# Batch 1's loads and w1 in one GpSimd queue; V_bf's evacuation and one norm placed elsewhere

## The chip, the core and the metric

The kernel runs on one core of a Trainium2 chip. The metric is the device time of one execution in microseconds (us). A core has a matrix engine (TensorE, PE in the profile), a vector engine (VectorE, DVE), an activation engine (ScalarE, ACT), a general engine (GpSimd, POOL) and a sync engine (SyncE, SP). Each works through its own instructions in program order and waits on semaphores for the others. Loads from HBM are moved by 16 DMA engines; here SP and GpSimd issue them, each into a queue of its own. On-chip data lies in SBUF, matrix results in PSUM.

## What is computed

Linear attention with cosine weights for 8 batches of 8 heads, 576 rows and 64 columns, and behind it a mixer: a low-rank mix over rows and a two-layer MLP over the 512 channels. The core of the reference:

```python
q_p = concat(relu(q) * cos_w, relu(q) * sin_w)      # k_p likewise
kv  = einsum('bhsf,bhsd->bhfd', k_p, v)
z   = sum(k_p, axis=2)
num = einsum('bhsf,bhfd->bhsd', q_p, kv)
den = einsum('bhsf,bhf->bhs', q_p, z) + 1e-06
x   = (num / den), heads side by side                # (8, 576, 512)
u   = x + (x^T @ U @ V)^T
out = u + relu(u @ w_ch1) @ w_ch2                    # w_ch1: 512 x 2048, w_ch2: 2048 x 512
```

## The kernel before

**Tiling.** The 576 rows of a batch are four blocks of 128 and a tail of 64. `load_main` (L74) loads the four blocks of q, k or v of a batch (1 MB), `load_tail` (L80) the tail (128 KB); both issue from SP unless an engine is given. `w1_load(n)` (L89) loads a quarter of w_ch1 from GpSimd's queue and turns float32 into bfloat16 on the way: 1 MB is read, 512 KB are written. Sixteen blocks j of 128 hidden channels use w1: j 0 to 3 the first quarter, 4 to 7 the second, and so on.

**Order.** The kernel uses a manual schedule: the order in which the Python code calls its helpers is the order of each engine's instructions. Batches 0 and 1 are written out by hand, the others come from a table (`PLAN`). For batch 0 and 1 the steps are:

- `q_prep`, `k_prep` (L248, L242): ReLU and cosine or sine scale, on DVE and ACT by a pair of engines; the results are `q_p`, `k_p` and for the tail `q_tl`, `k_tl`.
- `v_prep`, `v_block` (L208, L219): casts of v into `v_ext`.
- `qtr_unit` (L275): PE transposes q_p into PSUM, then a copy to `q_pT` or `q_tlT`.
- `kv_unit` (L254): kv for four heads. `den_unit` (L316): the denominators and their reciprocal (`rec0`, `rec1` for heads 0 to 3 and 4 to 7).
- `xh_unit` (L332): the numerators of four heads of one row block, and their norm: one DVE operation, or with an engine given four ACT activations of 64 columns each.
- `A_unit` (L383): x by U. `uTd_open`, `uTd_mm`, `uTd_evac` (L436 to L458): the transposed u, with the matrix `V_bf`.
- `g1_main(b, j)` (L481): four matmuls of w1's block j and a ReLU on ACT (`hid`). `g2_part` (L525): the second layer and the output.

`V_four` (L186) makes the matrix behind `V_bf` in PSUM (tag "X", one buffer, next used by `den_unit`), and `V_evac` (L198) copies it to SBUF. `chain0` (L657) holds batch 0 from its first kv to its first u; after it `chain_end` and the first `g1_main` calls follow, then `q_prep(1, 4)` and `q_prep(1, 0)`, and then the slots with what `at(j, ...)` (L763) puts beside block j.

**Loads around the change.** SP issues batch 0's loads at the start and then, in program order, batch 1's: q, q tail, k, k tail, v tail, v in two halves. No marker holds them; a buffer's readers do (`qst`, `qt`, `vst`, `vt` have one buffer, `kst` and `kt` two). GpSimd waits for v's first half by a small copy (`mark`, L738), issues w1's first quarter (L739), casts parts of v in `chain0` and issues the second quarter (L673). The third and fourth quarters (L773) wait for a second copy, of `q_tlT` (L772), and stand ahead of GpSimd's casts of batch 1's v; w2's four loads follow (L776). SP's loads for batch 2 wait for a one-element DMA of `rec1` (`mark2`, L707).

Of the kernel before, what the change touches and what calls it, by code (L numbers as in the profile page):

```python
# [17 lines left out]
def kernel(  # L18
# [11 lines left out]
    nc = tc.nc  # L30
# [12 lines left out]
    TS = 64  # L43
# [5 lines left out]
    def tail(b):  # L49
        lo = TS * (b % 2)  # L50
        return slice(lo, lo + TS)
# [8 lines left out]
    kst, vst, qst, kt, vt, qt = {}, {}, {}, {}, {}, {}  # L60

    def alloc_k(b):
        kst[b] = pool.tile([P, H, 4, D], FP32, tag="kst", bufs=2, name="kst")
        kt[b] = pool.tile([P, H, D], FP32, tag="kt", bufs=2, name="kt")

    def alloc_v(b):
        vst[b] = pool.tile([P, H, 4, D], FP32, tag="vst", bufs=1, name="vst")
        vt[b] = pool.tile([P, H, D], FP32, tag="vt", bufs=1, name="vt")

    def alloc_q(b):  # L70
        qst[b] = pool.tile([P, H, 4, D], FP32, tag="qst", bufs=1, name="qst")
        qt[b] = pool.tile([P, H, D], FP32, tag="qt", bufs=1, name="qt")

    def load_main(dst, src, b, h0=0, h1=H, eng=None):  # L74
        (eng or nc.sync).dma_start(  # L75
            out=dst[:, h0:h1, :, :].rearrange("p h c d -> p h (c d)"),
            in_=src[b, h0:h1, 0:512, :].rearrange("h (p c) d -> p h (c d)", c=4),
        )

    def load_tail(dst, src, b, h0=0, h1=H, eng=None):  # L80
        (eng or nc.sync).dma_start(  # L81
            out=dst[tail(b), h0:h1, :],
            in_=src[b, h0:h1, 512:S, :].rearrange("h s d -> s h d"),
        )
# [4 lines left out]
    def w1_load(n):  # L89
        cs = slice(n * 512, n * 512 + 512)  # L90
        nc.gpsimd.dma_start(
            out=w1_bf[:, :, cs], in_=moe_w_ch1.rearrange("(d p) n -> p d n", p=P)[:, :, cs]
        )

    def w2_load(n):
        js = slice(n * 4, n * 4 + 4)
        nc.gpsimd.dma_start(
            out=w2_bf[:, js, :], in_=moe_w_ch2.rearrange("(j p) n -> p j n", p=P)[:, js, :]
        )

    def cast(eng, o, i):
        if eng is nc.scalar:
            nc.scalar.activation(out=o, in_=i, func=AF.Copy, bias=0.0, scale=1.0)  # L103
        else:
            eng.tensor_copy(out=o, in_=i)  # L105


    V_, A_, G_ = nc.vector, nc.scalar, nc.gpsimd
# [5 lines left out]
        out=iota[:, 0:4], pattern=[[1, 4]], base=0, channel_multiplier=4,  # L114
        allow_small_or_imprecise_dtypes=True,
    )
    for lo in (0, TS):
        nc.gpsimd.iota(
            out=iota[lo : lo + TS, 4:5], pattern=[[1, 1]], base=512, channel_multiplier=1,
# [29 lines left out]
    q_tlT = const.tile([P, H, P], BF16)  # L149
# [10 lines left out]
        out=U_bf[:, 0:4, :], in_=moe_U[0:512, :].rearrange("(p c) r -> p c r", c=4)  # L160
# [15 lines left out]
    def keep_warm(n, tag, bufs):  # L176
        w_ps = ps.tile([P, 512], FP32, tag=tag, bufs=bufs, name="w_ps")
        for _ in range(n):
            nc.tensor.matmul(out=w_ps, lhsT=zero[:, 0:P], rhs=zero, start=True, stop=True)

    mark = const.tile([TS, 1], FP32)
    mark2 = const.tile([1, 1], FP32)
# [15 lines left out]
    def V_evac(eng):  # L198
        cast(
            eng, V_bf.rearrange("p c t -> p (c t)"),  # L200
            v4_ps[0].rearrange("p a n -> p (a n)")[:, 0 : 5 * P],
        )
# [5 lines left out]
    def v_prep(b, h0=0, h1=H, cs=range(5), engs=None):  # L208
        vx = v_ext[b % 2]
        for n, c in enumerate(cs):  # L210
            eng = engs[n] if engs else G_
            if eng is None:
                continue
            if c < 4:
                cast(eng, vx[:, c, h0:h1, 0:D], vst[b][:, h0:h1, c, :])
            else:
                cast(eng, vx[tail(b), 4, h0:h1, 0:D], vt[b][tail(b), h0:h1, :])

    def v_block(b, h0, h1, c0, c1, eng):  # L219
        cast(  # L220
            eng,
            v_ext[b % 2][:, c0:c1, h0:h1, 0:D].rearrange("p c h d -> p h c d"),
            vst[b][:, h0:h1, c0:c1, :],
        )
# [17 lines left out]
    def k_prep(b, c, engs, h0=0, h1=H):  # L242
        if b not in k_p:
            k_p[b] = pool.tile([P, 4, H, 2 * D], BF16, tag="k_p", bufs=1, name="k_p")
        src = kst[b][:, h0:h1, c, :] if c < 4 else kt[b][:, h0:h1, :]
        prep(k_p[b][:, c] if c < 4 else k_tl, src, b, c, engs, h0, h1)
# [55 lines left out]
    def qT_of(b, c, h):  # L302
        return q_pT[b][:, c, h, :] if c < 4 else q_tlT[:, h, :]

    def x_alloc(b):
        if b not in x_bf:
            x_bf[b] = pool.tile([P, 4, DM], BF16, tag="x_bf", bufs=2, name="x_bf")

    def x_of(b, c, rows=slice(0, P)):
        return x_bf[b][:, c, :] if c < 4 else x_tl[rows, :]  # L310
# [21 lines left out]
    def xh_unit(b, c, h0, h1, rec, tag, bufs, eng=None):  # L332
        x_alloc(b)
        n = h1 - h0
        rows = slice(0, P) if c < 4 else tail(b)
        acc = ps.tile([P, n, D], FP32, tag=tag, bufs=bufs, name="xh_ps")
        for h in range(h0, h1):
            nc.tensor.matmul(
                out=acc[:, h - h0, :], lhsT=qT_of(b, c, h), rhs=kv_sb[b][:, h, 0:D],
                start=True, stop=True,  # L340
            )
        if eng is not None:
            for h in range(h0, h1):
                eng.activation(
                    out=x_of(b, c, rows)[:, h * D : h * D + D], in_=acc[rows, h - h0, :],
                    func=AF.Copy, bias=0.0, scale=rec[rows, c, h - h0 : h - h0 + 1],
                )
            return
        nc.vector.tensor_tensor(
            out=x_of(b, c, rows)[:, h0 * D : h1 * D].rearrange("p (i d) -> p i d", d=D),  # L350
            in0=acc[rows],
            in1=rec[rows, c, :].unsqueeze(2).to_broadcast([P if c < 4 else TS, n, D]),
            op=ALU.mult,
        )
# [96 lines left out]
    def uTd_evac(b, d, eng):  # L451
        cast(eng, uT[b][:, :, d, :], uT_ps[b, d])
# [192 lines left out]
    O2, G3 = ("o", 2), ("g", 3)  # L645

    def chain_begin(b):
        u01 = ps.tile([P, 2, 512], FP32, tag="X", bufs=1, name="u01")
        for d in (0, 1):
            uTd_open(b, d, None, None, u01[:, d, :].rearrange("p (c t) -> p c t", c=4))  # L650
# [6 lines left out]
    def chain0():  # L657
        v_prep(0, 0, 4, (4,), (A_,))
        v_block(0, 0, 4, 0, 3, V_)
        v_block(0, 0, 4, 3, 4, A_)  # L660
        k_prep(0, 4, (A_, A_), 4, 8)
        kv_unit(0, 0, "T", 1)
        qtr_unit(0, 4, 0, H, V_, *G3)
        keep_warm(2, "o", 2)
        for c in (0, 1):
            k_prep(0, c, (V_, A_), 4, 8)
        rec0 = den_unit(0, 0, 4, "X", 1)
        for c in (2, 3):
            k_prep(0, c, (V_, A_), 4, 8)
        v_prep(0, 4, 8, (4,), (G_,))  # L670
        v_block(0, 4, 8, 0, 2, G_)
        v_block(0, 4, 8, 2, 4, A_)
        w1_load(1)  # L673
        for n, c in enumerate(TL):
            xh_unit(0, c, 0, 4, rec0, *(O2, O2, G3, G3, G3)[n], A_ if n == 1 else None)
        keep_warm(1, "X", 1)
        kv_unit(0, 1, "T", 1, A_)
        rec1 = den_unit(0, 4, 8, "X", 1)
        a0 = A_unit(0, "T", 1, A_, 0, 256)
        for n, c in enumerate(TL[:3]):  # L680
            xh_unit(0, c, 4, 8, rec1, *(O2, O2, G3)[n])
        chain_begin(0)
        uTd_mm(0, 0)
        uTd_mm(0, 1)
        for n, c in enumerate(TL[3:]):
            xh_unit(0, c, 4, 8, rec1, *G3)
        uTd_evac(0, 0, A_)
        uTd_evac(0, 1, A_)
        keep_warm(2, "o", 2)
        return a0  # L690
# [38 lines left out]
        if c in (1, 3):  # L729
            keep_warm(1, "X", 1)  # L730
    V_four("X", 1)
    V_evac(V_)
    for c in TL:
        k_prep(0, c, (V_, A_ if c < 3 else V_), 0, 4)
    q_prep(0, 4, (V_, A_))
# [2 lines left out]
    G_.tensor_copy(out=mark, in_=vst[0][0:TS, 0, 0, 0:1])  # L738
    w1_load(0)  # L739
    a0 = chain0()  # L740
    alloc_q(1)
    load_main(qst[1], q, 1)
    load_tail(qt[1], q, 1)
    alloc_k(1)
    load_main(kst[1], k, 1)
    load_tail(kt[1], k, 1)
    alloc_v(1)
    load_tail(vt[1], v, 1)
    load_main(vst[1], v, 1, 0, 4)
    load_main(vst[1], v, 1, 4, 8)  # L750
    chain_end(0, a0)
    g1_main(0, 0, True)
    uTd_close(0, 2, V_)
# [9 lines left out]
    def at(j, *thunks):  # L763
        beside.setdefault(j, []).extend(thunks)

    for n, c in enumerate(ORD):
# [2 lines left out]
        tg = ("T", 1) if n % 2 else O2  # L769
        at(1 + n, lambda c=c, tg=tg: qtr_unit(1, c, eng=V_, tag=tg[0], bufs=tg[1]))  # L770
        at((4, 5, 5, 6, 6)[n], lambda c=c, n=n: k_prep(1, c, (V_, A_)))
    at(2, lambda: G_.tensor_copy(out=mark, in_=q_tlT[0:TS, 0, TS : TS + 1]))  # L772
    at(2, lambda: [w1_load(2), w1_load(3)])  # L773
    at(2, lambda: v_prep(1, 0, H, (4,), (G_,)))
    at(2, lambda: v_block(1, 0, 4, 0, 4, G_))
    at(6, lambda: [w2_load(n) for n in range(4)])  # L776
    def fill1(n):
        if n in (0, 4):
# [68 lines left out]
```

## Time and profile before

| | |
|---|---|
| median of 5 runs | 319.78 us (319.3 to 321.72) |
| the profiled execution | 320.12 us, its span 318.2 us |
| PE busy | 308.5 us (97%) |
| DVE, ACT, POOL busy | 155.9 (49%), 151.4 (48%), 35.4 us (11%) |
| DMA queue of SP | 40.05 MB, 47.1% of 16 engines over the span |
| DMA queue of GpSimd | 11.35 MB, 14.9% |
| granted PE clock | 1.00 throughout |

The span runs from the first to the last instruction of the profiled execution; the device time holds some 1.9 us more. All instants below are us from the span's start. Where a view gives a wait in brackets, it is the idle time of that engine ahead of the instruction and what ended it. DMA-issuing instructions have their issue time in the timeline, not their transfer; "to landing" is counted from the issue.

In the first part of the program, PE is busy 7.57 us of the first 10, 8.85 of the next 10, 2.46 of the 4 up to 24, 9.00 of 9 up to 33, 5.76 of 7 up to 40, 29.68 of 30 up to 70. From 70 to 310 it is busy throughout. In the same stretches the DMA engines' busy share is 0.86, 1.07, 1.17, 1.17, 1.24 and 1.00.

### The profile page before, as it was taken

What the parts mean: (1) busy time and instruction counts of PE and PEld (TensorE: products, weight loads), DVE (VectorE), ACT (ScalarE), POOL (GpSimd) and SP (SyncE); (2) the same over time, 40 slices, a digit from 0 to 9 for tenths busy, and PEclk for the clock granted to TensorE, in tenths of its full rate; (3) what the DMA queues carried; (4) which work ended last, traced back from release to release, by engine and by line L of the source; (5) the groups of instructions that cost most, each with busy time, mean ns of one, the idle gap of its engine ahead of it and who ended that gap; (6) DMA issues with size and microseconds to landing.
All of it is one profiled execution on the core that took longest, in us unless ns stands there. A gap on an engine that the chain in (4) does not pass through costs nothing.

```text
span 318.2 us, 5795 instructions
## 1 busy us (share of the span) xinstructions
PE 308.5 (97%) x2380; PEld 161.9 (51%) x2380; DVE 155.9 (49%) x355; ACT 151.4 (48%) x261; POOL 35.4 (11%) x67
## 2 busy tenths in 40 slices
PE   7879899999999999999999999999999999999996
PEld 3545554475545444475455444574454444464443
DVE  8768754752877645037926484254736520001211
ACT  5848746685906256658400087559300166650000
POOL 4214400200121130000121100000121100000000
PEclk9999999999999999999999999999999999999999
DMA  7999999955286928960899369900691130001122
GB/s 217 292 266 273 207 222 336 334 180 186 71 207 156 312 68 180 249 217 2 193 265 329 140 137 223 345 11 33 146 197 71 68 82 0 2 0 68 66 88 77
DMA packets 83803, 51.82 MB, mean 163 GB/s; under 512 B 52066, under 2 KB 81026, under 8 KB 83778
## 3 DMA queue, kind: packets, MB, share of 16 engines
q1 hardware_dynamic: 76850, 40.05, 47.1%
q0 software_dynamic: 6784, 11.35, 14.9%
q8 instruction: 18, 0.29, 0.3%
q10 hardware_dynamic: 144, 0.07, 0.1%
q14 instruction: 7, 0.06, 0.1%
HBM read 36.86 MB, written 9.44 MB: 145 GB/s over the span
## 4 chain that ended last, share of the span: by engine, by line
PE 87%; DMA 6%; ACT 4%; SPq 1%; DVE 1%; issue 0%; POOL 0%; DVEq 0%; ACTq 0%
PE o_ps L543 39%; PE g_ps L491 33%; PE gt_ps L511 4%; DMA w_bf<-in_moe_w_ch_dram 3%; PE kv_ps L262 3%; PE va_ps L407 3%; PE x_ps L363 3%; DMA vst<-in_v_dram 2%; ACT hid L500 2%; PE a_ps L390 1%; PE t_ps L279 1%; ACT k_p L228 1%; SPq L81 1%; ACT q_p L228 1%; SPq L75 0%; PE d_ps L321 0%
## 5 line engine op out<-in xcount | busy, mean ns | idle before, releaser
L500 ACT ACTIVATE hid<-g_ps 128x512 bf16<-128x512 f32 x128 | 76.2, 596 | 100.8 <-PE g_ps L491 100.4
L491 PE MATMUL g_ps<-uT,w_bf 128*128 128x512 bf16 x512 | 118.5, 379 | 1.5 <-DMA w_bf<-in_moe_w_ch_dram 1.5
L543 PE MATMUL o_ps<-w_bf,hid 128*128 128x512 bf16 (+2 forms) x528 | 119.2, 373 | 0.0
L491 PEld LDWEIGHTS <-w_bf 128*128 128x128 bf16 x512 | 48.8, 98 | 57.4 <-DMA w_bf<-in_moe_w_ch_dram 1.7
L543 PEld LDWEIGHTS <-hid 128*128 128x128 bf16 x528 | 48.7, 98 | 52.8 <-issue 1.7
L553 DVE TENSOR_TENSOR o_sb<-u_bf,o_ps 128x512 f32<-128x512 bf16 (+2 forms) x33 | 22.0, 668 | 62.7 <-PE o_ps L543 62.6
L563 POOL DMA_DIRECT2D out_dram<-o_sb x24 | 13.5, 561 | 165.0 <-DVE o_sb L553 155.0
L408 DVE TENSOR_TENSOR u_bf<-x_bf,va_ps 128x512 bf16<-128x512 bf16 x32 | 21.7, 684 | 10.2 <-PE va_ps L407 10.1
L105 DVE CAST kv<-kv_ps 128x260 bf16<-128x260 f32 x14 | 6.0, 428 | 32.3 <-PE kv_ps L262 32.3
L373 DVE TENSOR_TENSOR x_bf<-x_ps,rec 128x512 bf16<-128x512 f32 x24 | 16.6, 691 | 0.8
L228 ACT ACTIVATE q_p<-qst,sinw 128x512 bf16<-128x512 f32 (+1 forms) x24 | 15.1, 657 | 2.2 <-DMA qst<-in_q_dram 2.1
L511 PE MATMUL gt_ps<-uT_tl,w_bf 128*128 128x128 bf16 x256 | 15.6, 219 | 0.0
L407 PE MATMUL va_ps<-A_sb,V_bf 128*128 128x512 bf16 x40 | 15.2, 379 | 0.0
L543 PE MATMUL o_ps<-w_bf,hid_tl 128*128 128x512 bf16 x64 | 15.1, 379 | 0.0
L313 DVE TENSOR_SCALAR rec<-x_ps 128x8 f32<-128x8 f32 (+1 forms) x30 | 4.9, 164 | 20.3 <-PE x_ps L363 20.2
L511 PEld LDWEIGHTS <-w_bf 128*128 128x128 bf16 x256 | 14.6, 98 | 0.5
L262 PEld LDWEIGHTS <-k_p 128*128 128x128 bf16 x256 | 11.5, 97 | 5.8 <-ACT v_ext L103 1.2
L230 DVE TENSOR_SCALAR k_p<-kst,cosw 128x512 bf16<-128x512 f32 (+1 forms) x31 | 14.3, 481 | 0.1
L262 PE MATMUL kv_ps<-v_ext,k_p 128*128 128x65 bf16 x256 | 12.5, 193 | 1.6 <-ACT k_p L228 0.9
L518 ACT ACTIVATE hid_tl<-gt_ps 128x512 bf16<-128x512 f32 x16 | 9.4, 597 | 5.5 <-PE gt_ps L511 5.5
L363 PEld LDWEIGHTS <-q_pT 128*128 128x128 bf16 x192 | 9.1, 98 | 5.5 <-issue 0.6
L103 ACT ACTIVATE v_ext<-vst 128x512 bf16<-128x512 f32 (+2 forms) x19 | 11.8, 636 | 0.1
(106 smaller groups left out, 253.2 us busy)
## 6 DMA issues: line engine op xcount, KB each, us to landing
qst<-in_q_dram SPq DMA_DIRECT2D x7, 1024.0 KB, 8.7
kst<-in_k_dram SPq DMA_DIRECT2D x7, 1024.0 KB, 7.6
vst<-in_v_dram SPq DMA_DIRECT2D x6, 1024.0 KB, 8.4
out_dram<-o_sb POOLq DMA_DIRECT2D x24, 256.0 KB, 3.4
w_bf<-in_moe_w_ch_dram POOLq DMA_DIRECT2D x8, 512.0 KB, 10.4
vst<-in_v_dram SPq DMA_DIRECT2D x4, 512.0 KB, 8.1
out_dram<-o_sb SPq DMA_DIRECT2D x7, 256.0 KB, 2.3
qst<-in_q_dram SPq DMA_DIRECT2D x2, 512.0 KB, 3.7
```

Source lines behind the costliest of these rows:

```text
L228: nc.scalar.activation(out=o, in_=i, func=AF.Relu, bias=0.0, scale=w)
L230: eng.tensor_scalar(out=o, in0=i, scalar1=0.0, scalar2=w, op0=ALU.max, op1=ALU.mult)
L262: nc.tensor.matmul(out=acc[:, i, :], lhsT=k_p[b][:, c, h, :] if c < 4 else k_tl[:, h, :], rhs=vx[:, c, h, :], start=(c == 0), stop=(c == 4),)
L363: nc.tensor.matmul(out=acc[:, g, i * E : i * E + E], lhsT=qT_of(b, c, h), rhs=kv_sb[b][:, h, :], start=True, stop=True,)
L373: nc.vector.tensor_tensor(out=x_of(b, c, rows).rearrange("p (g i d) -> p g i d", g=2, d=D), in0=view[:, :, :, 0:D], in1=rec[rows].unsqueez ...
L407: nc.tensor.matmul(out=va, lhsT=V_bf[:, c, :], rhs=A_sb[b], start=True, stop=True)
L408: nc.vector.tensor_tensor(out=u_bf[b][:, c, :] if c < 4 else u_tl[b // 2][rows, :], in0=x_of(b, c, rows), in1=va[rows, :], op=ALU.add,)
L491: nc.tensor.matmul(out=g_ps.rearrange("p (c t) -> p c t", c=4), lhsT=w1_bf[:, d, j * P : j * P + P], rhs=uT[b][:, :, d, :], start=(d == 0) ...
L500: nc.scalar.activation(out=hid[b][:, j, :], in_=g_ps, func=AF.Relu, bias=0.0, scale=1.0)
L511: nc.tensor.matmul(out=g_ps[:, jj, :], lhsT=w1_bf[:, d, j * P : j * P + P], rhs=uT_tl[pr][:, d, :], start=(d == 0), stop=(d == 3),)
L543: nc.tensor.matmul(out=o[:, cols], lhsT=lhs[:, j, c * P : c * P + P], rhs=w2_bf[:, j, cols], start=(j == 0), stop=(j == NJ - 1),)
L553: nc.vector.tensor_tensor(out=o_sb[:, cols], in0=u[:, cols], in1=o[:, cols], op=ALU.add)
```

## The change

Batch 1's main loads of q, k and v leave SP and go to GpSimd's queue, inside `chain0` after GpSimd's casts of batch 0's v, in the order q, w1's second quarter, k, v's first and second half, w1's third quarter. Their tails stay on SP, in the order q, k, v, behind a one-element DMA of `rec0`. The copy of `q_tlT` that held the third and fourth quarter is gone; the fourth quarter is issued at j = 6, behind GpSimd's casts of batch 1's v and ahead of w2. `V_evac` moves from behind `V_four` to behind DVE's cast of v in `chain0`. In the second half of the heads, the norm of row block 1 moves from DVE to ACT, as it already is in the first half. PE's instructions and their order are the same.

```diff
     def chain0():
         v_prep(0, 0, 4, (4,), (A_,))
         v_block(0, 0, 4, 0, 3, V_)
+        V_evac(V_)
         v_block(0, 0, 4, 3, 4, A_)
...
         v_block(0, 4, 8, 0, 2, G_)
         v_block(0, 4, 8, 2, 4, A_)
+
+        alloc_q(1)
+        alloc_k(1)
+        alloc_v(1)
+        load_main(qst[1], q, 1, eng=G_)
         w1_load(1)
+        load_main(kst[1], k, 1, eng=G_)
+        load_main(vst[1], v, 1, 0, 4, G_)
+        load_main(vst[1], v, 1, 4, 8, G_)
+        w1_load(2)
+
+        nc.sync.dma_start(out=mark2, in_=rec0[0:1, 0, 0:1])
+        load_tail(qt[1], q, 1)
+        load_tail(kt[1], k, 1)
+        load_tail(vt[1], v, 1)
         for n, c in enumerate(TL):
             xh_unit(0, c, 0, 4, rec0, *(O2, O2, G3, G3, G3)[n], A_ if n == 1 else None)
...
         for n, c in enumerate(TL[:3]):
-            xh_unit(0, c, 4, 8, rec1, *(O2, O2, G3)[n])
+            xh_unit(0, c, 4, 8, rec1, *(O2, O2, G3)[n], A_ if n == 1 else None)
...
     V_four("X", 1)
-    V_evac(V_)
     for c in TL:
         k_prep(0, c, (V_, A_ if c < 3 else V_), 0, 4)
...
     w1_load(0)
     a0 = chain0()
-    alloc_q(1)
-    load_main(qst[1], q, 1)
-    load_tail(qt[1], q, 1)
-    alloc_k(1)
-    load_main(kst[1], k, 1)
-    load_tail(kt[1], k, 1)
-    alloc_v(1)
-    load_tail(vt[1], v, 1)
-    load_main(vst[1], v, 1, 0, 4)
-    load_main(vst[1], v, 1, 4, 8)
     chain_end(0, a0)
...
-    at(2, lambda: G_.tensor_copy(out=mark, in_=q_tlT[0:TS, 0, TS : TS + 1]))
-    at(2, lambda: [w1_load(2), w1_load(3)])
     at(2, lambda: v_prep(1, 0, H, (4,), (G_,)))
     at(2, lambda: v_block(1, 0, 4, 0, 4, G_))
+    at(6, lambda: w1_load(3))
     at(6, lambda: [w2_load(n) for n in range(4)])
```

## The prediction

> **What bounds the kernel now.** I read the busy shares first: PE 308.5 of a span of 318.2 us, so at most 9.7 us can be won. The table of stretches then says where PE idles: 3.6 us in the first 20 us, 1.54 us from 20 to 24, nothing from 24 to 33, 1.24 us from 33 to 40, nothing from 70 to 310. The chain of waits over 12 to 30 us names the second of these:
>
> ```profile
> 4.97 7.91 DMA vst<-in_v_dram
> 12.88 0.05 issue
> 12.93 0.61 POOL mark L738
> 13.54 10.16 DMA w_bf<-in_moe_w_ch_dram
> 23.70 0.05 issue
> 23.75 0.60 PE g_ps L491 x2
> ```
>
> The first quarter of w1 is issued at 13.54 and lands at 23.70; PE had finished everything else at 22.27 and stood 1.48 us. The timeline of PE's weight loads shows this stop and the next one, a small one: the transposes of batch 1's q tail wait for ACT's half of q_tl.
>
> ```profile
> 23.74 0.11 PEld L491 LDWEIGHTS <-w_bf 128*128 128x128 bf16 x2 [1.65 <-DMA w_bf<-in_moe_w_ch_dram]
> ...
> 26.21 0.57 PEld L279 LDWEIGHTS <-q_tl 128*128 128x128 bf16 x8 [0.20 <-ACT q_tl L228]
> ```
>
> Why w1 is slow is in the DMA view, by windows. In order: 14 to 17 us (SP's queue q1 alone), 18 to 25 (both queues), 33 to 40 (GpSimd's q0 alone), 45 to 45.9 (after SP issued k's tail of batch 2 at 42.67):
>
> ```profile
> q1 hardware_dynamic: 1035, 1.02, 102.8%
> ...
> q0 software_dynamic: 836, 0.84, 70.7%
> q1 hardware_dynamic: 1004, 0.83, 44.8%
> ...
> q0 software_dynamic: 1455, 1.44, 124.0%
> ...
> q0 software_dynamic: 185, 0.19, 125.4%
> ```
>
> Columns are packets, MB, share of the 16 engines. Alone, SP's queue moves 0.34 MB/us of float32 and GpSimd's 0.207 MB/us of w1 (written as bfloat16). Together each gets 0.12 MB/us. So w1's first quarter (0.52 MB) needs 2.5 us alone and about 4.4 beside batch 1's q, k and v. It also joined late: no q0 packet before 17.3 us, 3.8 us after its issue. A store of 75.63, with nothing else moving, had its first traffic 1.1 us after issue; another, issued at 102.77 into a busy SP queue, had none until 107 (4.3 us). The last line is the reverse case: SP's queue, which joined a busy GpSimd queue, had no packet for 3.3 us.
>
> The consumers, from the timelines of DVE, ACT and SP:
>
> ```profile
> 25.33 0.49 DVE L230 TENSOR_SCALAR q_tl<-qt,cosw 64x512 bf16<-64x512 f32 x1
> ...
> 20.52 1.09 ACT L103 ACTIVATE uT<-u 128x512 bf16<-128x512 f32 x2 [0.97 <-PE u L456]
> ...
> 25.45 0.72 ACT L228 ACTIVATE q_tl<-qt,sinw 64x512 bf16<-64x512 f32 x1
> ...
> 41.87 0.75 SPq L707 DMA_DIRECT2D mark<-rec  x1
> ```
>
> From 24.6 to 34.6 DVE has no gap worth naming, and ACT has one, 0.45 us before 30.05. Both take their work in program order, and q_tl is near its head.
>
> [...] eight w1 and w2 issues took 0.75 to 0.80 us each, some beside DVE casts. [...]
>
> **The change, step by step.** Sums are against the profiled execution (320.12 us, span 318.2), 0.34 above the median of 319.78.
>
> 1. V_bf's evacuation (DVE, 0.82 us) leaves 9.87, where DVE then stood until k landed at 10.77: nothing won. It goes behind v's cast, which ends at 13.56, and would end at 14.38; the next DVE work, kv, started at 14.41 when PE was done. Cost 0 to 0.1; I take 0. The cover is 0.85 us wide; without it the whole 0.82 would fall on kv. Its PSUM buffer is next needed at 15.09.
>
> 2. A second norm goes to ACT: four activations, 0.89 us (row of 16.46), in the 0.97 us that ACT waits before 20.52. It removes 0.41 us from DVE, but the fourth norm's matmuls end at 20.6 anyway, so the last DVE norm gains at most 0.05. I take 0 (bounds -0.1 to +0.1).
>
> 3. w1's first quarter has the engines to itself. SP's batch-0 loads end about 13 to 15 us; q0 needs 1.1 us from issue, so it starts at 14.65, moves 2.5 us, and lands 1.5 to 2 us later: 19 to 20. (A third quarter issued at 28.04 started at 30.7 and landed at 34.74, 1.5 us beyond its transfer.) PE needs it at 22.27: the 1.48 us stop goes.
>
> 4. What is late next. Main parts in GpSimd's queue: q is issued at 16.54 behind the v cast, then w1's second quarter, k, v in halves, w1's third: six issues of 0.75 to about 1 us, done by 22 with nothing urgent behind them on POOL. A float32 packet has half the source bytes of a w1 packet, so I take SP's rate, 3.0 us per MB. Including the tails (0.13 MB each, near 0.45 us) transfers end: q 20.6, w1 23.6, k 27, v 28.5 and 30.2, w1 32.7. Landing 2 us later compares with the present need so: q 22.6 (25.85), w1 25.6 (28.94), k 29 (31.2), v 30.5 and 32.2 (kv really starts 35.1 after k_p; ACT takes the rest at 35.45), w1 34.7 (36.98). All have 1.5 us or nearly so.
>
> 5. The tails are the weak step. SP's marker waits for rec0 (ends 16.26): 0.75 us, so q's tail is issued at 17.1. It now joins a busy queue: first packet at 20.4 to 21.4 by the three delays above, 18.2 if it is idle just then. Its 512 packets take turns with w1's, of which q0 passed 836 in 7 us beside SP's queue, 119 a us: 4.3 us, or 3.8 if it catches the end of q; beside q's shorter packets about 2. Landing: lowest 18.2+2+2 = 22.2, highest 21.4+4.3+1 = 26.7; I take 20.9+3.8+0.5 = 25.2. PE's transposes start 0.81 us (0.72 of ACT and two hand-overs) after that: 26.0 against 26.21. So 1.48 us won at w1 shrink to 0.2 at q_tl, and ACT and DVE, full from there, pass that on. k's and v's tails come near 28 and 30.5, POOL's casts need them at 30.0: 0.5 late, under cover of k_p.
>
> Sum: 0 + 0 - 1.48 + 1.28 = -0.2: 319.9 for this execution, 319.6 for the median. DVE and ACT are the new limit.
>
> **Rivals.**
>
> - *The whole stop is won.* If q's tail lands by 23.9 (26.21-1.48-0.81) all shifts by 1.48. The third quarter of w1 then has 0.8 us of slack, so 0.2 to 0.5 may be lost there: -1.2, 318.6. For it: marker and q's tail reach the engines at nearly the same moment as q itself. Against: three of three joins were late.
>
> - *The tails starve (slower).* In the last DMA line above SP's queue got nothing while GpSimd's was full, and first packets at 45.9 came as that queue ran dry. If this is not a delay but a rule, q's tail waits behind q, w1 and k. Each us beyond 25.4 stops PE, DVE and ACT alike by one us: 1.6 us of loss from a landing at 27.0. With 29 it is 29+0.81-26.21 = +3.6, 323.4. Against: at 18 to 25 us two full queues shared evenly.
>
> - *GpSimd's float32 packets are as dear as its w1 packets.* From the lines above a packet of w1 takes 1.24 x 7 x 16 / 1455 = 95 ns of an engine, one of SP's 48. At 95 a MB costs 3 us more: v's first half lands near 38, kv 3 us late and w1's third quarter at 43 for 36.98: about +5, 325. Against: a store by this queue (75.63) moved its 0.26 MB in about 0.7 us, so the queue itself is not slow.
>
> **How the numbers follow.** Little net change 0.49 (own range 318.9 to 320.6), whole stop won 0.24, starving tails 0.20, dear packets 0.07. 0.5%, 1.6 us, is about what a measurement can tell from no change: below 318.2 or above 321.4. The stop alone is worth 0.46%, so only the best of the second case counts as faster: 0.1. Slower is both last cases less a little of the mild one: 0.26. Same: 0.64. The range needs 0.8: 318.3 leaves out about 0.1 below, 323.0 about as much above.
>
> **What would show it.** PE's first g_ps at 22.3 instead of 23.75 shows step 3 right; a wait before it, wrong. The wait ahead of the q_tl transposes growing from 0.2 to more than 1 us, ended by ACT q_tl, shows step 5; if it stays at 0.2 and they start before 25, the first rival holds. A wait of kv_ps for v_ext, or of g_ps for w_bf near 36, means step 4's rates are wrong. DVE's kv of batch 0 after 14.5 would refute step 1. The forecast fails if the tails' landing leaves 23.9 to 27.

## The result, and the profile after

The changed kernel took 321.74 us (median of 29 executions, 319.94 to 324.86), the kernel before 319.85 us on the same chip (50 executions, 318.18 to 323.43). The ratio is 1.0056, 95% interval 1.0036 to 1.0076: slower by about 1.8 us, where 319.6 us, no change, was forecast. The profiled execution took 322.65 us, 2.5 us more than that of before; its span is 320.9 us, 2.7 us more.

PE's timeline of the changed kernel, with the waits ahead of its instructions in brackets, answers to the stops shown before:

```profile
22.20 0.59 PE L491 MATMUL g_ps<-uT,w_bf 128*128 128x512 bf16 x2
...
26.03 0.62 PE L279 MATMUL t_ps<-ident,q_tl 128*128 128x128 bf16 x8 [1.07 <-ACT q_tl L228]
...
35.74 0.54 PE L262 MATMUL kv_ps<-v_ext,k_p 128*128 128x65 bf16 x4 [2.12 <-POOL v_ext L105]
37.29 0.57 PE L321 MATMUL d_ps<-kv,q_pT 128*128 128x1 bf16 x16 [0.30 <-DVE kv L105]
37.82 1.87 PE L491 MATMUL g_ps<-uT,w_bf 128*128 128x512 bf16 x4
```

The stop for w1's first quarter is gone: g_ps starts at 22.20 instead of 23.75, with no wait. The transposes of q_tl start at 26.03; their weight loads start at 26.03 too, 0.2 before the 26.21 of the kernel before. So far all is as forecast. Then batch 1's first kv waits 2.12 us for `v_ext`, a wait that before did not have. PE's timeline of before at the same place:

```profile
34.52 0.20 PE L262 MATMUL kv_ps<-v_ext,k_p 128*128 128x65 bf16 x1 [0.53 <-ACT k_p L228]
35.13 0.20 PE L262 MATMUL kv_ps<-v_ext,k_p 128*128 128x65 bf16 x1 [0.41 <-ACT k_p L228]
36.34 0.54 PE L321 MATMUL d_ps<-kv,q_pT 128*128 128x1 bf16 x16 [0.30 <-DVE kv L105]
36.84 1.02 PE L491 MATMUL g_ps<-uT,w_bf 128*128 128x512 bf16 x4
```

There kv followed k_p piece by piece, and the denominators (d_ps) began at 36.34; after the change they begin at 37.29, 0.95 later. The chain of waits of the changed kernel from 20 to 40 us says what released kv:

```profile
20.68 0.75 POOL w_bf L91
21.43 12.52 issue
33.95 0.02 POOLq L105
33.97 0.01 issue
33.97 0.62 POOL v_ext L105
34.59 0.05 issue
34.65 1.05 POOL v_ext L105
35.70 0.04 issue
35.74 1.04 PE kv_ps L262 x20
```

GpSimd stood idle for 12.5 us, then cast v's tail (0.62) and v's first half (1.05). Its timeline names what it waited for:

```profile
33.97 0.61 POOL L105 CAST v_ext<-vt 64x512 bf16<-64x512 f32 x1 [12.54 <-DMA vt<-in_v_dram]
34.65 1.04 POOL L105 CAST v_ext<-vst 128x1024 bf16<-128x1024 f32 x1
```

Before the change the same cast of v's tail ran at 30.04:

```profile
30.04 0.83 POOL L105 CAST v_ext<-vt 64x512 bf16<-64x512 f32 x1 [0.50 <-DMA vt<-in_v_dram]
```

V's tail landed at 33.9. V's first half, 512 KB on the other queue, had landed at 31.6 and waited 2.3 us more behind the tail's cast, which stands ahead of it in GpSimd's program. SP had issued the three tails one behind the other:

```profile
17.26 0.66 SPq L81 DMA_DIRECT2D qt<-in_q_dram  x1
17.96 0.63 SPq L81 DMA_DIRECT2D kt<-in_k_dram  x1
18.77 0.90 SPq L81 DMA_DIRECT2D vt<-in_v_dram  x1
```

They landed 8.0, 12.0 and 15.1 us after these instants, at 25.3, 30.0 and 33.9.

The second half of the loss is in the last line of PE's timeline above: four matmuls of w1 take 1.87 us after the change and 1.02 before. In the windows of 1 us from 37 to 42 of the changed kernel (columns: PE, PEld, DVE, ACT, POOL busy with the number of instructions, granted PE clock, DMA share, GB/s):

```profile
37.00:38.00 1.00, 0.71 (x21) 0.64 (x21) 0.82 (x3) 0.00 (x0) 1.00 (x3) 0.63 0.35 32
38.00:39.00 1.00, 1.00 (x3) 0.30 (x2) 0.46 (x2) 0.00 (x0) 1.00 (x2) 0.50 1.13 186
39.00:40.00 1.00, 1.00 (x11) 0.67 (x10) 0.06 (x1) 0.27 (x1) 0.35 (x1) 0.50 1.24 203
40.00:41.00 1.00, 1.00 (x7) 0.37 (x5) 0.79 (x2) 0.32 (x1) 0.00 (x0) 0.67 1.11 165
41.00:42.00 1.00, 1.00 (x30) 0.88 (x29) 0.52 (x2) 0.60 (x1) 0.00 (x0) 1.00 1.15 190
```

The clock missing in these lines is 0.37 + 0.50 + 0.50 + 0.33, so 1.7 us of full clock, which is half clock for 3.4 us, from about 37.3 to 40.7. At most 1.7 us of work is lost so. A later fixed point says how much: the matmuls of batch 1's transposed u (uT_ps, L456) start at 49.64 after the change and at 47.24 before, 2.40 later. The wait accounts for 0.95 of that, and the other 1.45 are put down to the clock. From 70 to 310 us PE is busy 239.93 of 240, so nothing is made good, and these 2.4 us are nearly all that the two profiled executions differ by (2.5 us, 2.7 by span).

Over all executions, 22 of 29 of the changed kernel had a mean granted clock below 0.998, with a median of 322.20 us, against 320.59 for the other 7.

### The profile page after: what moved, and what is told of

Its sections match the earlier page's. It is cut to its first block, busy times and chain, and to the rows that moved or that the text cites. A ratio compares the mean times of both kernels' runs of the same rounds, so it can differ in the third digit from the quotient of the medians.

```text
span 320.9 us, 5802 instructions
## 1 busy us (share of the span) xinstructions
PE 310.9 (97%) x2380; PEld 162.8 (51%) x2380; DVE 154.5 (48%) x354; ACT 152.4 (48%) x265; POOL 38.1 (12%) x70
## 4 chain that ended last, share of the span: by engine, by line
PE 85%; issue 4%; DMA 3%; POOL 2%; ACT 2%; SPq 1%; DVE 1%; POOLq 0%; DVEq 0%
PE o_ps L543 39%; PE g_ps L491 31%; PE gt_ps L511 4%; PE kv_ps L262 3%; PE va_ps L407 3%; DMA vst<-in_v_dram 3%; PE x_ps L363 2%; PE a_ps L390 1%; ACT hid L500 1%; POOL v_ext L105 1%; ACT q_p L228 1%; SPq L81 1%; PE t_ps L279 1%; POOL w_bf L91 0%; POOL vst L75 0%
## 5 line engine op out<-in xcount | busy, mean ns | idle before, releaser
L491 PE MATMUL g_ps<-uT,w_bf 128*128 128x512 bf16 x512 | 119.7, 382 | 0.0
L228 ACT ACTIVATE q_p<-qst,sinw 128x512 bf16<-128x512 f32 (+1 forms) x24 | 15.1, 657 | 2.2 <-DMA qst<-in_q_dram 2.1
L543 PE MATMUL o_ps<-w_bf,hid_tl 128*128 128x512 bf16 x64 | 15.1, 379 | 0.0
L511 PEld LDWEIGHTS <-w_bf 128*128 128x128 bf16 x256 | 14.6, 98 | 0.5
L230 DVE TENSOR_SCALAR k_p<-kst,cosw 128x512 bf16<-128x512 f32 (+1 forms) x31 | 13.2, 447 | 1.5 <-DMA kst<-in_k_dram 1.5
L179 PE MATMUL w_ps<-zero 128*128 128x512 bf16 x35 | 11.4, 466 | 1.2 <-DVE U_bf L162 1.2
L103 ACT ACTIVATE v_ext<-vst 128x512 bf16<-128x512 f32 (+2 forms) x19 | 11.8, 636 | 0.5 <-DMA vst<-in_v_dram 0.4
```

What stands on the lines that cost most here:

```text
L228: nc.scalar.activation(out=o, in_=i, func=AF.Relu, bias=0.0, scale=w)
L230: eng.tensor_scalar(out=o, in0=i, scalar1=0.0, scalar2=w, op0=ALU.max, op1=ALU.mult)
L491: nc.tensor.matmul(out=g_ps.rearrange("p (c t) -> p c t", c=4), lhsT=w1_bf[:, d, j * P : j * P + P], rhs=uT[b][:, :, d, :], start=(d == 0) ...
L511: nc.tensor.matmul(out=g_ps[:, jj, :], lhsT=w1_bf[:, d, j * P : j * P + P], rhs=uT_tl[pr][:, d, :], start=(d == 0), stop=(d == 3),)
L543: nc.tensor.matmul(out=o[:, cols], lhsT=lhs[:, j, c * P : c * P + P], rhs=w2_bf[:, j, cols], start=(j == 0), stop=(j == NJ - 1),)
```

## Why the tails landed late

The DMA view of the changed kernel in the window from 26 to 31 us, when k and v ran in GpSimd's queue q0 and the tails in SP's queue q1 (packets, MB, share of the 16 engines):

```profile
q0 software_dynamic: 504, 1.88, 93.9%
q1 hardware_dynamic: 503, 0.13, 11.4%
```

The packets are even, 504 against 503, as many as if each queue had one in turn. The bytes are not. 1.88 MB in 504 packets is 3.7 KB a packet, though a row of this load is 1 KB (from 19 to 21 us, with no packet of SP's queue, 151 packets held 0.61 MB, 4.0 KB each); SP had moved the same rows in packets of 1 KB (1.02 MB in 1035 packets, in the prediction). A tail's row is 256 bytes, and each tail has 512 of them. So for each 3.7 KB packet on the other queue the tail moves 256 bytes, and at 503 packets in 5 us its 512 packets take 5 us. By the shares, a packet of GpSimd's queue held an engine for 149 ns here (0.939 x 5 us x 16 / 504), where the prediction had worked out 48 ns for one of SP's. The forecast had about 2 us for a tail "beside q's shorter packets": it took a float32 packet of GpSimd's queue to be as short as SP's.

Two earlier windows of the same view, 21 to 23 us and 23 to 26 us, show that turns are not the whole story:

```profile
q0 software_dynamic: 208, 0.45, 79.1%
q1 hardware_dynamic: 550, 0.14, 33.1%
...
q0 software_dynamic: 436, 0.53, 89.5%
q1 hardware_dynamic: 423, 0.11, 27.0%
```

SP's queue had only 2 packets between 16 and 21, so q's tail waited about 4 us from its issue. Then, as q's own transfer ended in GpSimd's queue (its packets held 3.7 KB from 21 to 22 and 1.1 KB, as w1's do, from 22 to 23), SP's queue moved 550 packets to GpSimd's 208: q's tail passed in a burst, not by turns. From 23 to 26 the queues were even again, and by count most of k's tail passed there, beside w1's second quarter; v's tail came beside the 3.7 KB packets.

## The experiments

All ratios are to the kernel before on the same chip, with 95% intervals; "full clock" counts the executions with a mean granted clock of 0.998 or more. In the kernel before these were 156 of 238 over the five groups of runs.

| run | ratio | full clock |
|---|---|---|
| changed kernel, first | 1.0056 [1.0036, 1.0076] | 7 of 29 |
| changed kernel, second | 1.0073 [1.0045, 1.0101] | 2 of 10 |
| changed kernel, third | 1.0053 [1.0027, 1.0078] | 3 of 14 |
| v's tail in GpSimd's queue | 1.0027 [1.0004, 1.0049] | 11 of 21 |
| v's first half cast first | 1.0020 [1.0000, 1.0041] | 11 of 20 |
| 12 idle matmuls ahead of kv | 1.0033 [1.0012, 1.0055] | 21 of 21 |
| v's tail there, 6 idle matmuls | 1.0024 [1.0001, 1.0047] | 18 of 21 |
| the same, q's tail there too | 0.9996 [0.9970, 1.0021] | 13 of 14 |
| tails issued behind batch 0 | 0.9993 [0.9968, 1.0019] | 9 of 14 |
| all tails in GpSimd's queue | 1.0061 [1.0037, 1.0086] | 1 of 11 |
| half the packets in the tails | 0.9982 [0.9958, 1.0007] | 15 of 22 |
| small edits alone | 1.0018 [0.9998, 1.0039] | 10 of 22 |
| loads alone, first | 1.0135 [1.0103, 1.0166] | 0 of 6 |
| loads alone, second | 1.0076 [1.0051, 1.0101] | 2 of 14 |
| before, 6 idle matmuls | 1.0007 [0.9984, 1.0029] | 17 of 22 |
| tails and q early | 1.0006 [0.9983, 1.0028] | 11 of 21 |
| the same, 6 idle matmuls | 0.9979 [0.9959, 0.9998] | 15 of 22 |

### The wait for v

**V's tail in GpSimd's queue**, ahead of v's first half.

```diff
         load_main(kst[1], k, 1, eng=G_)
+        load_tail(vt[1], v, 1, eng=G_)
         load_main(vst[1], v, 1, 0, 4, G_)
...
-        load_tail(vt[1], v, 1)
```

> The changed kernel, with v's tail issued from GpSimd's queue just ahead of v's first half instead of last on SP. Theory A (what costs the time is the late tail of v: GpSimd's casts of batch 1's v stand in order behind it, so kv waits 2.1 us, and PE's clock then falls for the pause): v's tail lands with v's first half near 31.7 us, kv starts near 34.8 us behind k_p, the clock stays at 1.00; 319.4 to 319.9 us, 0.5 to 0.7% faster than the changed kernel. Theory B (the 4 KB packets of q, k and v from GpSimd's queue, or the late third quarter of w1, cost the time, not the tail): 321 us or more, and PE still waits before kv or before g_ps near 37.

By the median half of it came: 1.0027. (The intervals of this run and of the next two overlap that of the changed kernel, which ran on other chips. What each cure does is read from its trace and its clock count; the time alone does not tell the three from the changed kernel.) The tail now landed 12.2 us after its issue, with v, and kv's wait for v_ext fell from 2.12 to 1.03 us, with kv following k_p again at 33.70. But in the profiled execution the clock still fell after that pause, to 0.76 over 33 to 40 us.

**V's first half cast first.** GpSimd's two casts of batch 1's v are exchanged; the loads stay.

```diff
-    at(2, lambda: v_prep(1, 0, H, (4,), (G_,)))
     at(2, lambda: v_block(1, 0, 4, 0, 4, G_))
+    at(2, lambda: v_prep(1, 0, H, (4,), (G_,)))
```

> The changed kernel with GpSimd's two casts of batch 1 swapped: v's four blocks first, v's tail behind them. Theory A: the large cast runs when v's first half lands (31.6 us), only the short one (0.6 us) waits for the tail at 33.9, so kv starts near 34.8 to 35 instead of 35.74; the pause of PE is 1.4 us instead of 2.1 and the clock may hold: 319.9 to 320.8 us. Theory B (the wait is not for the tail but for v's main part or for GpSimd itself): kv near 35.7 and 321.7 us as in the changed kernel.

PE's timeline of this run:

```profile
25.98 0.62 PE L279 MATMUL t_ps<-ident,q_tl 128*128 128x128 bf16 x8 [1.85 <-ACT q_tl L228]
34.16 0.20 PE L262 MATMUL kv_ps<-v_ext,k_p 128*128 128x65 bf16 x1 [0.53 <-ACT k_p L228]
34.77 0.20 PE L262 MATMUL kv_ps<-v_ext,k_p 128*128 128x65 bf16 x1 [0.41 <-ACT k_p L228]
```

The wait for v_ext is gone though v's tail is as late as ever (15.9 us from issue): what held kv was the order of two casts behind a late tail. The 1.0020 says that this is again only a part; the first line shows the other late tail still in place.

**Idle matmuls.** `keep_warm` puts matmuls on zeros ahead of batch 1's first kv; 12 instead of 2.

```diff
-    at(7, lambda: keep_warm(2, "X", 1))
+    at(7, lambda: keep_warm(12, "X", 1))
```

> The changed kernel with 12 instead of 2 idle matmuls of zeros (0.216 us each) ahead of batch 1's first kv, where PE stood 2.1 us; the wait for v itself stays. Theory A2 (of the loss of 2.4 us at 50 us, some 1.4 come from the half clock that PE was granted from 37.6 to 40.6 after the pause): kv still starts near 35.7, the clock is 1.00 throughout, and the time falls to 320.3 to 320.9 us. Rival (the half clock has another cause, such as load on the chip, or costs nothing in the end): clock low as before and 321.5 to 322 us.

The clock behaved as expected: 21 of 21 executions at full clock, against 7 of 29. The time did so only in part: 1.0033. The late tail itself was still there: in the profile the idle matmuls ended at 34.4, and kv waited another 0.23 us for v_ext and began at 34.61. The median of 321.37 is above the expected 320.3 to 320.9, but the kernel before was 0.6 us slower on this chip than on the first (320.41 against 319.85).

**Both together**, with 6 idle matmuls.

> V's tail in GpSimd's queue ahead of v's first half, as in the first experiment (1.0027), and 6 idle matmuls in place of 2 ahead of batch 1's first kv, as a milder form of the fourth (1.0033). Theory: the late tail of v and the half clock behind the pause are the two terms of the loss; with both out the ratio is 0.999 to 1.001, and executions with a clock below 0.998 are rare. Rival: the loss has a third term that neither touches (the wait for q's tail, or the late start of w1's and w2's loads); then the ratio stays at 1.002 or more.

The rival fits better: 18 of 21 at full clock, no wait of PE for v_ext, and still 1.0024, though the interval begins at 1.0001. In this run PE waited 1.42 us for q_tl and the transposes began at 26.78, against 26.35 before. That gives back the stop won at w1; it is not clearly a loss against before, as batch 0 ran 0.6 us later in this profile (w1's first issue at 14.13 against 13.54). So a third term is likely, not shown.

**Q's tail too.** As the run above, with q's tail in GpSimd's queue directly behind q; k's tail alone stays on SP.

```diff
         load_main(qst[1], q, 1, eng=G_)
+        load_tail(qt[1], q, 1, eng=G_)
...
-        load_tail(qt[1], q, 1)
```

> The previous run, which measured 1.0024 [1.0001, 1.0047] (v's tail in GpSimd's queue, 6 warm matmuls), with q's tail in GpSimd's queue too, directly behind q; only k's tail stays on SP. In the previous run's profile PE still waited 1.4 us for q_tl. Theory: that wait is the third term of the loss; q's tail lands near 23 as it did when all tails were in this queue, k's tail, now alone on SP, lands near 24, q_tl is not waited for, and the ratio is 0.997 to 1.000. Rival: the 1.5 us won ahead of q_tl end at k_p, ahead of which k's tail or k itself (one issue later) is now late; then kv starts no earlier and the ratio stays at 1.001 to 1.003.

```profile
25.72 0.62 PE L279 MATMUL t_ps<-ident,q_tl 128*128 128x128 bf16 x8 [0.65 <-ACT q_tl L228]
34.50 0.20 PE L262 MATMUL kv_ps<-v_ext,k_p 128*128 128x65 bf16 x1 [0.25 <-ACT k_p L228]
```

These lines of PE's timeline show the wait for q_tl at 0.65 (expected none: q was issued at 16.69, and its tail landed at 24.9 instead of 23) and kv held by k_p alone, for 0.25. The ratio is 0.9996, inside what was expected. Its interval and that of the changed kernel on this chip (1.0053) do not meet, so with both late tails and the clock mended the loss is gone. That q's tail is a third term is less firmly shown: 0.9996 and 1.0024 are from two chips, and their intervals overlap.

### Whether the tails' packets are the cause

**Half the packets**, beside the changed kernel on the same chip. Only heads 0 to 3 of batch 1's tails are loaded; the rest of the tail buffers is set to zero.

```diff
+        for t in (qt[1], kt[1], vt[1]):
+            G_.memset(t[tail(1), 4:8, :], 0.0)
...
-        load_tail(qt[1], q, 1)
-        load_tail(kt[1], k, 1)
-        load_tail(vt[1], v, 1)
+        load_tail(qt[1], q, 1, 0, 4)
+        load_tail(kt[1], k, 1, 0, 4)
+        load_tail(vt[1], v, 1, 0, 4)
```

> The changed kernel with only heads 0 to 3 of batch 1's three tails loaded; heads 4 to 7 of the tail buffers are set to zero by GpSimd behind its last issue, so this part of the computation is left out. 256 instead of 512 packets a tail, issued at the same instants, GpSimd's queue untouched. Theory (the two queues take turns packet by packet, and the tails' 256-byte packets pass at about 100 a us beside 4 KB packets): each tail needs 2.6 us instead of 5.2, so q's tail lands about 2.5 us earlier, near 22.5 us, and v's about 7.5 us earlier, near 26; the waits for q_tl and for v's tail go, and the time is 0.3 to 0.6% below the changed kernel on this chip. Rival (a queue that joins late is held back until the other's work is done, whatever it has to move): q's tail still lands near 25 and v's near 33 to 34, and the time is that of the changed kernel.

> The changed kernel a third time, the partner of the two others on this chip: 1.005 to 1.008 of before, q's tail near 25, v's near 33.5.

GpSimd's timeline of the changed kernel in this group, at v's tail, and under it that of the run with half the packets:

```profile
32.41 0.61 POOL L105 CAST v_ext<-vt 64x512 bf16<-64x512 f32 x1 [11.98 <-DMA vt<-in_v_dram]
```

```profile
27.73 0.61 POOL L105 CAST v_ext<-vt 64x512 bf16<-64x512 f32 x1 [6.06 <-DMA vt<-in_v_dram]
```

From issue to landing, q's, k's and v's tail took 6.6, 10.4 and 14.7 us with all packets and 6.6, 8.4 and 9.4 with half of them. Their issues lie 0.7 to 0.8 us apart, so the landings of successive tails lie 4.5 and 5.1 us apart with 512 packets and 2.5 and 1.8 with 256. The steps shrink by 44 and 65% with the packets: the second and third tail are held by what the tails have to move, not by a queue held back whatever it carries. (This run halves bytes and packets together; that packets count, and not bytes, is read from the 504 to 503 above.) The first tail did not gain: it took 6.6 us either way, where the theory had 2.5 less. Most of its time is that of joining: in both runs SP's queue had next to no packets between 18 and 20 us (5 and 2) while GpSimd's moved 156 and 152. This is one pair of profiles; in the others with q's tail on SP behind the marker it took 6.8 to 10.7 us.

The time went to 0.9982, against 1.0053 for the changed kernel on the same chip, with intervals that do not meet. So the landing of the tails is the cause of the loss. The gain over the changed kernel, 0.7%, is above the expected 0.3 to 0.6%. In this changed kernel q's and v's tail landed at 22.8 and 32.4, earlier than expected, and kv's wait for v_ext was 2.53 us.

**The tails early.** The marker (the one-element DMA of `rec0` ahead of the tails) is removed; SP issues the tails right behind batch 0's loads, from 11.8 to 14.6 us.

```diff
-        nc.sync.dma_start(out=mark2, in_=rec0[0:1, 0, 0:1])
         load_tail(qt[1], q, 1)
```

> The changed kernel without the marker, so that SP issues the three tails right behind batch 0's loads, before GpSimd's queue has anything. Theory A: q's tail lands before 20 and v's before 22, so neither q_tl nor GpSimd's casts wait; PE starts g_ps at 22.2, the transposes of q_tl near 24.7, kv of batch 1 near 33.5, and the whole stop of 1.5 us at w1 is won: 318.2 to 318.8 us, 0.3 to 0.5% below the kernel before. Theory B (order and queue of the main loads cost the time): 320.5 to 322 us, about the changed kernel.

Issued before GpSimd's queue was full, the tails landed 4.5 to 5.6 us after their issues, all before 21 us, and the loss vanished: 0.9993. In the profiled execution kv's two waits for k_p stood at 33.14 and 33.75, 1.4 us earlier than before's, as the full recovery of the first stop asks. The expected gain over the kernel before is not in the ratio.

**All tails in GpSimd's queue**, each behind its main load (v's ahead of it), without a marker.

> The changed kernel without the marker and with all three tails in GpSimd's queue, in the order q, q tail, w1's second quarter, k, k tail, v tail, v. Theory A (the tails are late because on SP they get one 256-byte packet for each 4 KB packet of GpSimd's queue): in one queue each lands with its neighbours, q's tail near 23.5, v's tail below 31; q_tl and GpSimd's casts do not wait for them, kv of batch 1 starts by 34, and 318.8 to 319.8 us. Rival (the tails' 256-byte packets cost the engines the time, wherever they are queued): v's first half still lands near 31.6, kv near 35, and 320.5 us or more.

A miss, 1.0061. Q's tail was mended (6.3 us). But the loads of GpSimd's queue landed here in the order of their issue (q at 22.8, its tail at 23.2, w1's second quarter at 25.9, k at 30.2), and k's tail behind k at 30.7. DVE's timeline:

```profile
30.66 0.49 DVE L230 TENSOR_SCALAR k_tl<-kt,cosw 64x512 bf16<-64x512 f32 x1 [2.99 <-DMA kt<-in_k_dram]
```

k_tl stands ahead of all k_p in program order, so kv ran from 33.4 to about 35.9 behind a late k_p, and only 1 of 11 executions kept the full clock. This is why k's tail was left on SP above. The rival's numbers came as well (over 320.5 us, v's first half at 32.2), so this run alone does not refute it; the run above with q's and v's tail in this queue, at 0.9996, speaks against it.

### The two small edits

**The small edits alone**: the kernel before with only `V_evac` and the norm moved.

> The kernel before with the two small edits alone; the loads stay. Theory A: both are hidden, 0.998 to 1.002 of the kernel before, w1's first quarter still stops PE near 22.3 for some 1.5 us. Rival (V_bf's evacuation delays batch 0's kv, or ACT's norm delays u's transposes): 1.003 or more.

1.0018 [0.9998, 1.0039]: at most a little loss, and not one that this measurement tells from none. The stop at w1 that was expected is not in this profile: PE's mean granted clock was 0.83 from 10 to 20 us (13 idle matmuls at 11.70 took 4.66 us, as many at 10.33 in the first run of the loads alone 2.97), batch 0 ran 2.3 us later, and w1 was there by the time PE came to it (24.44).

**The loads alone**: the changed kernel with both small edits undone, twice.

> The changed kernel with the two small edits undone: V_bf evacuated behind its matmuls, the second norm of row block 1 on DVE; only the loads are changed. Theory A: the loads carry the whole loss, so this is within 0.2% of the changed kernel, 1.004 to 1.007 of the kernel before, with the waits at q_tl and at kv as there. Rival (the small edits cost part of it): 1.003 or less.

> The new loads without the two small edits (V evacuated in its old place ahead of batch 0's k_p, all norms on VectorE), for the second time. Theory: with V evacuated early, VectorE's half of batch 0's k_p waits for V's product, so rec0 and the marker write end 0.5 to 1 us later against GpSimd's own issues, and q's tail joins a busier set of queues: it lands at 26.5 to 28.5 us, and the kernel is 0.4 to 0.9% slower than the changed kernel on this chip (1.010 to 1.014 of before). Rival: the first measurement (1.0135) was an accident of its chip; then both are within 0.2% of each other, and q's tail lands near 25.

> The changed kernel once more, as the partner of the next run on the same chip. It measured 1.0056 [1.0036, 1.0076] of before; I expect 1.003 to 1.008. In its profile q's tail should land 6.5 to 9 us after its issue at about 17.2 us, near 25, and v's tail near 33 to 34.

The first time it gave 1.0135, in six executions. Its profile had a very late tail of q; PE's timeline:

```profile
29.07 0.62 PE L279 MATMUL t_ps<-ident,q_tl 128*128 128x128 bf16 x8 [4.01 <-ACT q_tl L228]
```

I took that for the work of the small edits: V's early evacuation, which waits for V's product, held DVE's k_p, hence rec0 and the marker, and q's tail joined later. With the changed kernel beside it the theory fell: 1.0076 against 1.0073, q's tail 8.8 and 8.1 us from issue. The small edits make no difference that these runs show. The trace of the first time shows what was different in its profile: q landed at 23.3 there as in the changed kernel, but its tail came 5.0 us after q, at 28.3, where it came 2.0 after it in the changed kernel (25.3). Why it was so late, and whether it was in the other five executions, is open.

### Whether the clock alone, or an earlier q, gives a gain

**The kernel before with 6 idle matmuls.**

> The kernel before with 6 idle matmuls in place of 2 ahead of batch 1's first kv. On the last two chips 25 of 64 and 12 of 47 executions of before had a granted clock under 0.998 and took 1.15 to 1.6 us longer. Theory: that clock loss follows TensorE's pauses for k_p at 33.9 to 36.3 us; then nearly every execution here has a clock of 0.998 or more, and the median is 0.0 to 0.3% below before. Rival: it follows the stop for V near 9 us, or others; then the share of lower clocks stays at a quarter to a third and the time within 0.1%.

The share at full clock rose from 39 of 58 to 17 of 22, too little to tell, and the time did not change.

**Tails and q early**, then the same with 6 idle matmuls: as with the tails early, and q's main load issued right behind w1's first quarter.

```diff
     w1_load(0)
+    alloc_q(1)
+    load_main(qst[1], q, 1, eng=G_)
     a0 = chain0()
```

> The version without a marker, with q's main load issued right behind w1's first quarter, ahead of GpSimd's casts of batch 0's v. In the version without a marker q_p waited for q, issued at 16.75 and landed at 24.88. Theory A: q is issued near 13.6 and lands by 22.5, q_p does not wait, the casts of v are up to 0.9 us later but under cover; 0.3 to 0.6% below the kernel before. Rival (other waits, of k_p behind ACT's ReLUs and of v, bound the stretch anyway, so an earlier q is worth nothing): 0.998 to 1.001 as without a marker.

> The loads of the earlier run with the tails issued behind batch 0 and q's load behind w1's first quarter, with 6 idle matmuls ahead of batch 1's first kv. Theory: that run's executions at full clock took 318.87 us, those below 320.70; if the warm matmuls keep the clock up, nearly all are near 318.9, so 0.995 to 0.998 of before. Rival: the lower clocks come from elsewhere (the first loads), or the added matmuls cost as much as they save, as 12 of them did with v's tail late; then 0.999 to 1.002.

The first gave 1.0006; its 11 executions at full clock have a median of 318.87 us, the 10 others 320.70. The second gave 0.9979 [0.9959, 0.9998], the one version, with all work done, whose interval lies below the kernel before and all three runs of the changed kernel: 319.27 against 319.87 us. The gain is 0.2%, at the edge of what these runs can tell, and 7 of 22 executions still lost clock. In its profiled execution the loss lay elsewhere: after a pause of 1.14 us for v in batch 0 that ended at 17.3, the clock was 0.50 from 19 to 22.

## Why the prediction was wrong, point by point

- **Steps 1 and 2 held.** DVE's kv of batch 0 started at 14.51, V_bf ahead of it (13.57, 0.82 long). That is 0.1 later than before and on the line of the prediction's sign (14.5), but the cast of v ahead of both was 0.09 later too (13.10 against 13.01). ACT's new norm took 0.93 us in its wait. Alone, both edits showed no difference that can be told.
- **Step 3 held**: g_ps at 22.20, the stop of 1.48 us gone.
- **Step 4 held within 2 us.** Landings measured and (forecast): q 23.3 (22.6), w1's second quarter 27.4 (25.6), k 30.2 (29), v 31.6 and 33.1 (30.5 and 32.2), w1's third 35.4 (34.7). None of them ended a wait of PE. The sign that the prediction had set for wrong rates in this step, a wait of kv for v_ext, did come, but through v's tail.
- **Step 5, first part, held, with luck in the number.** Q's tail was forecast to land at 25.2 and the transposes to start at 26.0; it was 25.26 and 26.03. The stop won at w1 did shrink to 0.2. But the parts of the sum were off and made up for one another: first packets at 21.5 and not 20.9, about 1.4 us for the 512 packets and not 3.8, and 2.4 us from there to landing and not 0.5. In other profiles of these loads the same tail landed from 22.8 to 28.3.
- **Step 5, last sentence, failed**: "k's and v's tails come near 28 and 30.5, POOL's casts need them at 30.0: 0.5 late, under cover of k_p." They came at 30.0 and 33.9. The mechanism, tails that take turns with a full queue, was an estimate from w1's 836 packets in 7 us beside 1004 of SP's; it fits these two (423 packets beside 436, then 503 beside 504). The term that was mis-sized is the time that each further tail adds. The forecast had 2.8 and 2.5 us from one landing to the next, and 4.7 and 3.9 were measured. For v's tail the premise that failed is the author's estimate that a float32 packet of GpSimd's queue "has half the source bytes of a w1 packet" (no trace of before had one of these loads): these packets are 3.7 KB and not 1 KB, and 512 packets beside them take 5 us, not 2. K's tail was late for another reason as well: w1's second quarter still moved until about 25.5, where step 4 had 23.6, and k's tail passed beside it (423 packets to 436 from 23 to 26). Two tails later the error had become 3.4 us. The cover of k_p reached to 34.8, where ACT's last k_p ended; less the two casts (0.62 and 1.05) and the hand-overs the tail was needed by about 33.0, and the 0.9 beyond that fell on kv.
- **A term was missing from the sum**: the clock. The prediction put nothing on it. A pause of 2.12 us ahead of kv was followed by 3.4 us at half clock, about 1.45 us lost, more than the 0.95 that the wait itself cost.
- **The rivals.** "The tails starve" had the sign and the place of the trouble right, but put the price on q's tail (a landing at 29 us, 323.4). "As dear as its w1 packets" was off the other way: GpSimd's queue moved float32 at 0.376 MB a us, faster than the 0.34 of SP's. A packet did hold an engine longer than one of w1's (149 ns against 95), but it carried 3.7 KB, and these long packets are what the tails had to wait for.

What stays open: the earlier kv of the versions with early tails (1.4 us in a profile) is hardly found in their medians. Single profiles differ by more than a us in how batch 0's loads land, and no run here separates that. One part of it can be seen: the stop at w1 that was to be won is not the same in each execution of the old loads. It was 1.48 us in the profile of before, 0.51 in that of before with 6 idle matmuls, and absent in that of the small edits alone, where batch 0 was late. The forecast rested on one execution; how often the stop is that long was not counted.

## What to carry to other kernels

When loads move to GpSimd's queue, look at what is left on SP beside them, and count packets and not bytes: while both queues were busy here, the small-row loads got one short packet for every long one of the other queue (503 of 256 bytes beside 504 of 3.7 KB), and each further one in the row landed 4.7 and 3.9 us after the one ahead of it. Follow every small load to the cast that uses it, and to what stands behind that cast in program order. Put a term for the clock into the price of a new PE pause: here one of 2.1 us cost 0.95 us by itself and about 1.45 more by the clock, which was low in 22 of 29 executions.

## What the runs showed of the hardware

- GpSimd's queue packed 1 KB rows of float32 into packets of 3.7 KB on average (1.88 MB in 504) and moved 0.376 MB a us beside the tails; SP's alone moved the same rows in 1 KB packets at 0.34 MB a us.
- Two busy queues moved nearly the same number of packets: 504 and 503 in 5 us, 436 and 423 in 3 us. It was not so just when a transfer ended in GpSimd's queue: 208 to SP's 550 in 2 us.
- A first small load beside a busy GpSimd queue still had next to no packets 3.3 to 3.8 us after its issue: issued at 17.26, SP's queue moved 2 up to 21 (changed kernel); issued at 16.16 and 16.68, it moved 5 and 2 from 18 to 20 (changed kernel, third; half the packets). In one pair of profiles it landed 6.6 us after issue with 256 packets and 6.6 with 512; in other profiles with 512 it took up to 10.7.
- In the changed kernel's profile PE's clock fell to 0.50 about 1.5 us after the end of a pause of 2.12 us and stayed there for 3.4 us. Ten profiles of this case show a lower clock in their first 70 us. The clock missing there adds up to 1.7 us of full clock in nine of them (0.24 x 7 us in three, from 33 to 40) and to 1.9 in the tenth, where 0.9 of it is read from one rounded mean over 30 us. With idle matmuls in the pause 21 of 21 executions kept the full clock; without, 7 of 29.
- The length of one pause did not tell it here: a profile with a pause of 1.85 us kept the full clock (loads alone, second), and one with pauses of 0.53 and 0.41 us lost it (half the packets).
